# Attention's last weight block decoded and stored in round 22 instead of round 23, and its last four weight splits placed behind the first unit of the linear layers

## Chip, cores and metric

The kernel runs on one core of a Trainium2 chip. The metric is the device time of one execution in microseconds (us); less is better. The engines of the core have their own instruction queues: PE or TensorE (matmuls), DVE or VectorE, ACT or ScalarE, POOL or GpSimd, and SP, which here only issues DMA transfers, each in program order.

## What is computed

```python
S, D = 448, 64                      # 8 batches, 12 heads
scores = q @ k.transpose(0, 1, 3, 2) / sqrt(D) - log(S)
attn   = 1 / (1 + exp(-scores))     # a sigmoid, no sum over keys
x = (attn @ v).transpose(0, 2, 1, 3).reshape(3584, 768)
h = maximum(maximum(x @ w1, x @ w2), x @ w3)
out = h @ w_out                     # all weights 768 x 768
```

Inputs are float32, the weights float64 words that the kernel decodes to float32 itself.

## The kernel before

**Attention** (L277 to 466) handles one group of four heads a round, 24 rounds in all (n = 0 to 23, the loop at L420). A round takes about 10.17 us of TensorE: scores of the second head pair, scores of the next round's first pair (only if there is a next round, `ahead`), and the products with v, which gather in two PSUM banks, ps_av0 and ps_av1; the next round copies these to SBUF and stores them in x_dram (`finish`, L377).

**Weights.** The first layer weights are multiplied in a form with seven products in place of eight, so each needs sums of its blocks (a11 to a22, s1 to s4), and every operand goes in as a high and a low part. Attention does part of this work in the background. The generator `decoding` (L161) holds 24 blocks (0 to 23): for each of three weights four blocks of stage 0, which stay on the chip, and four of stage 1, which go to w_dram. A call decodes one block: two operations on ScalarE (L180, L181), four on DVE (L182 to L191). A stage 1 block is decoded in one call, and with `late=True` its store is issued at the start of the next, ahead of the next decode. Raw blocks rotate through 3 buffers, decoded ones (wb) through 2. `split_weights` (L407) makes the high and low part of one sum by a cast and a subtraction on DVE. In the round, L446 and L447 call both: one split (two in round 22), then one decode. So block 23 is decoded in round 23 and its store issued after the loop (L465), that of block 22 in round 23. The splits of the third weight become possible in round 20, and there are seven (order s3, a22, s1, a11, s2, a12, s4): one each in rounds 20 and 21, two in 22, one in 23, and two behind the first unit of the linear layers (L618).

In the last round t_store (L443) writes four token sums of 672 KB each to DRAM, and the high and low part of the first operand b11 are made (x_hi on ScalarE, L269; x_lo on DVE, L273).

**Linear layers** (L472 on). When attention ends, its pools are freed and new pools take their memory: xo2, which holds the high and low parts of the other six token operands (5376 bytes a partition each, in the order t2, t3, t1, b21, t4, b22, high before low), then c and dec2. The old memory began with dec: 3 raw buffers of 3072 bytes, 2 decoded ones of 1536, then the squares (2 x 1792), qk, hl, v, a. A tile of a new pool waits for the last use of the old tiles under it. Four visits (token pairs) for each of four stages, each of three units (q = 0 to 2), make 48 units; a unit is seven products of nine matmuls (three terms by three blocks of 128), some 12.6 us. The operands t2, t3, t1 of the first unit are made at L532 to L533, those of its last three products within it. Unit 0 of visit 0 uses the first weight, unit 2 the third.

All instructions keep program order on their engine (`pin`), so what is queued ahead of an instruction on its engine delays it.

Of the kernel before, what the change touches and what calls it, by code (L numbers as in the profile page):

```python
# [39 lines left out]
def attention_then_maxout(  # L40
# [86 lines left out]
    def w_stage():  # L127
        return {name: ws_p.tile([P, HP], F32, name=f"ws_{name}") for name in BLOCKS}
# [13 lines left out]
    def w_combine(r, names):  # L142
        for name in names:
            r[name] = r["a21"] if name == "s3" else ws_p.tile([P, HP], F32, name=f"ws_{name}")
            in0, in1, op = W_SUMS[name]
            pin(nc.gpsimd.tensor_tensor(out=r[name], in0=r[in0], in1=r[in1], op=op))  # L146
# [9 lines left out]
    def w_split(q, name, r, copy):  # L156
        hi, lo = w_tiles(q, name)
        pin(copy(out=hi, in_=r[name]))
        pin(nc.vector.tensor_tensor(out=lo, in0=r[name], in1=hi.bitcast(F32), op=ALU.subtract))

    def decoding(dec_p, todo, bufs, ahead, square_p, late=False):  # L161

        raws = []

        def load(st, q, n):
            col = (st if st < 3 else q) + 3 * (n // 2)
            src = w123[q, col] if st < 3 else wout[col]
            raw = dec_p.tile([P, HALF, P], I64, name="wraw", bufs=ahead)
            r = n % 2
            pin(nc.sync.dma_start(out=raw, in_=src[:, r * HALF : (r + 1) * HALF]))  # L170
            return raw

        def decode(raw, out):

            words = raw.bitcast(U32).rearrange("p a (c two) -> p (a c) two", two=2)
            low, high = words[:, :, 0], words[:, :, 1]
            square = square_p.tile([P, S], F32, name="c")[:, :HP]
            bits = dec_p.tile([P, HP], U32, name="wb", bufs=bufs)
            out = bits.bitcast(F32) if out is None else out
            pin(nc.scalar.activation(out=square, in_=high.bitcast(F32), func=AF.Square))  # L180
            pin(nc.scalar.activation(out=low, in_=low, func=AF.Copy, scale=2.0**-29))  # L181
            pin(nc.vector.tensor_scalar(  # L182
                out=bits, in0=high, scalar1=3, scalar2=0x3FFFFFF8,
                op0=ALU.logical_shift_left, op1=ALU.bitwise_and,
            ))
            pin(nc.vector.scalar_tensor_tensor(
                out=bits, in0=high, scalar=0xC0000000, in1=bits,
                op0=ALU.bitwise_and, op1=ALU.bitwise_or,
            ))
            pin(nc.vector.tensor_tensor(out=bits, in0=bits, in1=low, op=ALU.add))  # L190
            pin(nc.vector.scalar_tensor_tensor(  # L191
                out=out, in0=square, scalar=LEAST**2, in1=bits.bitcast(F32),
                op0=ALU.is_ge, op1=ALU.mult,
            ))
            return out

        for k, (st, q, n) in enumerate(todo):
            while len(raws) < min(k + ahead, len(todo)):
                raws.append(load(*todo[len(raws)]))
            if k == 0:  # L200
                yield
            if st == 0:
                if n == BLOCKS.index(W_ORDER[0][0]):
                    stage = w_stage()
                decode(raws[k], stage[BLOCKS[n]])
                w_combine(stage, dict(W_ORDER)[BLOCKS[n]])
                yield q, stage
            else:
                bits = decode(raws[k], None)
                if late:  # L210
                    yield
                pin(nc.sync.dma_start(out=w_dram[st, q][:, n], in_=bits))
                if not late:
                    yield


# [32 lines left out]
    def t_store(r, p):  # L249
        for k, name in enumerate(TOKENS):  # L250
            pin(nc.sync.dma_start(out=t_dram[p][:, k], in_=r[name]))
# [25 lines left out]
    def attention(stack):  # L277
# [11 lines left out]
        todo = []  # L289
# [3 lines left out]
        background = decoding(dec_p, todo, 2, 3, sq_p, late=True)  # L293
        splits = []

        def decode():
            done = next(background)
            if done:
                q, stage = done
                decoded.append(q)  # L300
                if decoded.count(q) == len(BLOCKS):
                    splits.extend((q, name, stage) for name in W_SPLITS)
# [8 lines left out]
        def load_v(b, f):  # L311
            t = v_p.tile([P, 14, D], F32, name="v")
            pin(nc.sync.dma_start(out=t, in_=v[b, f]))
            return t

        def sigmoid(ps):
            a = a_p.tile([P, 2, S], F32, name="a")
            pin(nc.scalar.activation(  # L318
                out=a, in_=ps[:, :, :S], func=AF.Sigmoid, bias=bias_s, scale=scale
            ))  # L320
            return a[:, 0], a[:, 1]

        def qk_split(t):

            hi = hl_p.tile([P, 2 * S], F32R, name="hi")
            lo = hl_p.tile([P, 2 * S], F32R, name="lo")
            pin(nc.vector.tensor_copy(out=hi, in_=t))
            pin(nc.vector.tensor_tensor(out=lo, in0=t, in1=hi.bitcast(F32), op=ALU.subtract))
            return (hi, hi), (hi, lo), (lo, hi)
# [42 lines left out]
        def load(n, pair):  # L372
            if n < len(fours):
                b, f = fours[n]
                return load_qk(b, 2 * f + pair)
# [26 lines left out]
        def raw_sigmoid(a):  # L402
            pin(nc.scalar.activation(
                out=a[1], in_=a[1], func=AF.Sigmoid, bias=bias_s, scale=scale
            ))

        def split_weights(most=1):  # L407
            for _ in range(most):
                if splits:
                    w_split(*splits.pop(0), nc.vector.tensor_copy)  # L410

        xs, count, pss = {}, len(fours), None
# [7 lines left out]
        for n in range(count):  # L420
            ahead = n + 1 < count
            later_ts = [later_t, load(n + 2, 1)]
            later_t = load(n + 3, 0)
            if ahead:
                next_vt = load_v(*fours[n + 1])
            if n == 0:
                first_terms = qk_split(next_ts[0])
            finish(n - 1, pss, gs=(0,))
            second = [shared_scores(scores(second_terms, c), c) for c in range(C)]
            finish(n - 1, pss, gs=(1,))  # L430
            if ahead:
                second_terms = qk_split(next_ts[1])
            next_first = []
            for c in range(C - 1):
                if ahead:
                    next_first.append(sigmoid(scores(first_terms, c)))
                raw_sigmoid(second[c])
            raw_sigmoid(second[C - 1])
            last_ps = scores(first_terms, C - 1) if ahead else None
            if n + 2 < count:  # L440
                first_terms = qk_split(later_ts[0])
            if n == count - 1:
                t_store(xs, 0)  # L443
                for name in FIRST:
                    x_lo(*x_hi(name, xs))
            split_weights(2 if n == count - 2 else 1)  # L446
            decode()  # L447
            if ahead:
                next_first.append(sigmoid(last_ps))

            part = n - 9
            if 0 <= part < 4 * HALF:
                k, block = divmod(part, 4)
                row, th = ((0, 1), (0, 0), (1, 1), (1, 0))[block]
                x_block(xs, x_dram, 0, row, th, k)
                x_combine(xs, ((), ("t1",), ("t2", "t3"), ("t4",))[block], (k,))
            pss = [ps_av.tile([P, 512], F32, name=f"ps_av{g}") for g in range(2)]
            for g, weights in enumerate((first, second)):
                for c in range(C):
                    weigh(pss[g], vt, g, c, weights[c])  # L460
            next_last = sigmoid(last_scores(next_ts)) if ahead else None
            last_weigh(pss, vt, last)
            if ahead:
                vt, first, next_ts, last = next_vt, next_first, later_ts, next_last
        next(background, None)  # L465
        return xs, lambda *to: finish(len(fours) - 1, pss, *to), split_weights

    with ExitStack() as stack:
        xs, finish, split_weights = attention(stack)
# [56 lines left out]
    ]  # L526
    todo = [(st, q, n) for st in (2, 3) for q in range(3) for n in range(4)]
    background = decoding(dec_p, todo, 1, 2, c_p)


# [137 lines left out]
```

## Time and profile before

| | us |
|---|---|
| median of 3 runs (872.13 to 872.5) | 872.45 |
| the profiled execution | 871.14 |
| its span, first to last instruction | 869.1 |
| busy: TensorE | 854.5 (98%) |
| busy: DVE | 658.0 (76%) |
| busy: ScalarE | 411.3 (47%) |
| busy: GpSimd | 177.0 (20%) |

The profile is one execution, recorded by the hardware. Its page groups instructions by line and tiles; beside it the trace can be asked for the waits (who waited for whom), for a timeline of an engine, for stretches of time, and for the instructions of one line or tile. In a timeline a row has the start in us from the span's start, the length, the engine, line and operation, the tiles (out<-in, without numbers, so that xhi_t is that of t1, t2, t3 or t4), and in brackets the idle time of the engine before it and what ended it. Operations on one engine are pipelined, so that the next may start a little before the end of the one before. A releaser is inferred from semaphores, and a wait for several is put down to the one that came last. In a stretch the columns are its length, then the busy time and count of PE, of weight loads, DVE, ACT and POOL, the granted clock of TensorE as a share of its full 2.4 GHz, the DMA engines' busy share and GB/s. Instructions of a line or tile are listed with count, least, median and greatest length in ns, and first and last start.

### The profile page before, as it was taken

To read this page: it belongs to the slowest core of one execution; us is meant where nothing else is said; L and a number is where in the kernel's file an instruction comes from. 1 tells how busy PE (TensorE), PEld (TensorE's weight loads), DVE (VectorE), ACT (ScalarE), POOL (GpSimd) and SP (SyncE) were. 2 spreads that over 40 slices of the span, in tenths; PEclk is the share of its full clock that TensorE was granted. 3 is DMA by queue.
4 is the path that set the end of the run, shared out by engine and by line. 5 is a ranking of instruction groups with operands and counts; after the bars stand their busy time and mean duration, and the time that the engine had idled before them with its cause. 6 is when DMAs were issued, how large, how long until landed. Compare 5 with 4: busy or idle time off the path is not lost. (4 is left out here: it accounts for less than half of the span.)

```text
span 869.1 us, 13093 instructions
## 1 busy us (share of the span) xinstructions
PE 854.5 (98%) x4842; PEld 698.8 (80%) x4842; DVE 658.0 (76%) x947; ACT 411.3 (47%) x571; POOL 177.0 (20%) x148
## 2 busy tenths in 40 slices
PE   7999999999979999999999999999999999999998
PEld 4555555555539999999999999999999998999997
DVE  5888888888857848589696888869688798837452
ACT  6888877788852414242253444225334352423320
POOL 0100012112002562602100020210002453760600
PEclk9999999999989999999999999999999999999999
DMA  7667776777654464414846542483663416262412
GB/s 269 224 225 252 235 242 237 258 262 245 201 203 172 168 233 147 187 52 131 307 141 236 219 171 79 135 304 134 239 230 138 168 58 230 82 213 98 169 73 84
DMA packets 74479, 161.88 MB, mean 186 GB/s; under 512 B 6960, under 2 KB 53936, under 8 KB 74416
## 3 DMA queue, kind: packets, MB, share of 16 engines
q1 hardware_dynamic: 74272, 160.94, 52.4%
q8 instruction: 38, 0.62, 0.3%
q14 instruction: 25, 0.20, 0.1%
q10 hardware_dynamic: 144, 0.11, 0.0%
HBM read 109.90 MB, written 51.12 MB: 185 GB/s over the span
## 5 line engine op out<-in xcount | busy, mean ns | idle before, releaser
L482 PE MATMUL ps_y<-xlo_t,whi_s 128*128 128x448 f32 x432 | 157.4, 364 | 4.3 <-DVE xlo_t L273 4.3
L482 PE MATMUL ps_y<-xhi_t,wlo_s 128*128 128x448 f32 x432 | 157.2, 364 | 1.5 <-ACT xhi_t L269 1.5
L482 PE MATMUL ps_y<-xhi_t,whi_s 128*128 128x448 f32 x432 | 156.7, 363 | 0.0
L318 ACT ACTIVATE a<-ps_s,bias_s 128x896 f32<-128x896 f32 x96 | 96.3, 1005 | 37.9 <-PE ps_s L348 33.3
L482 PE MATMUL ps_y<-xhi_b,wlo_a 128*128 128x448 f32 x288 | 104.5, 363 | 0.0
L482 PE MATMUL ps_y<-xlo_b,whi_a 128*128 128x448 f32 x288 | 104.4, 362 | 0.0
L482 PE MATMUL ps_y<-xhi_b,whi_a 128*128 128x448 f32 x288 | 104.0, 361 | 0.0
L592 ACT COPY p<-ps_y 128x448 f32<-128x448 f32 x48 | 25.5, 531 | 157.1 <-PE ps_y L482 156.6
L146 POOL TENSOR_TENSOR ws_s<-ws_a,ws_a 128x384 f32<-128x384 f32 x12 | 12.5, 1041 | 408.4 <-DVE u L598 172.7
L482 PEld LDWEIGHTS ps_y<-xlo_t,whi_s 128*128 128x128 f32 x432 | 81.6, 189 | 9.4 <-DVE xlo_t L273 4.6
L482 PEld LDWEIGHTS ps_y<-xhi_t,wlo_s 128*128 128x128 f32 x432 | 81.5, 189 | 7.8 <-ACT xhi_t L269 1.9
L482 PEld LDWEIGHTS ps_y<-xhi_t,whi_s 128*128 128x128 f32 x432 | 81.4, 188 | 5.7
L566 DVE TENSOR_TENSOR m<-ps_y,u 128x448 f32<-128x448 f32 x71 | 43.8, 620 | 52.6 <-PE ps_y L482 51.1
L273 DVE TENSOR_TENSOR xlo_t<-xs_t,xhi_t 128x1344 fp32r<-128x1344 f32 x42 | 67.9, 1616 | 4.0 <-DMA w_dram<-wb 4.0
L238 POOL TENSOR_TENSOR xs_t<-xs_b,xs_t 128x448 f32<-128x448 f32 x48 | 64.3, 1364 | 31.9 <-DMA xs_b<-x_dram 31.3
L595 DVE TENSOR_TENSOR u<-ps_y,p 128x448 f32<-128x448 f32 x48 | 29.8, 622 | 53.6 <-PE ps_y L482 48.4
L564 ACT COPY m<-ps_y 128x448 f32<-128x448 f32 x24 | 12.8, 534 | 120.9 <-PE ps_y L482 110.2
L273 DVE TENSOR_TENSOR xlo_b<-xs_b,xhi_b 128x1344 fp32r<-128x1344 f32 x42 | 68.0, 1620 | 2.4 <-ACT xhi_b L269 2.4
L269 ACT CAST xhi_t<-xs_t 128x1344 fp32r<-128x1344 f32 x42 | 55.3, 1317 | 17.7 <-PE ps_y L482 8.6
L180 ACT ACTIVATE c<-wraw 128x384 f32<-128x384 f32 x48 | 26.7, 557 | 74.7 <-DVE m L572 42.6
L269 ACT CAST xhi_b<-xs_b 128x1344 fp32r<-128x1344 f32 x42 | 55.3, 1318 | 9.9 <-PE ps_y L482 9.9
L356 PE MATMUL ps_av<-a,v 128*64 128x448 f32 x288 | 59.4, 548 | 0.0
(71 smaller groups left out, 1787.4 us busy)
## 6 DMA issues: line engine op xcount, KB each, us to landing
qk<-qk SPq DMA_DIRECT2D x48, 448.0 KB, 4.1
xs_b<-x_dram SPq DMA_DIRECT2D x30, 672.0 KB, 6.9
wraw<-w SPq DMA_DIRECT2D x36, 384.0 KB, 5.0
xs_t<-t_dram SPq DMA_DIRECT2D x18, 672.0 KB, 7.9
v<-v SPq DMA_DIRECT2D x24, 448.0 KB, 5.8
h_dram<-m SPq DMA_DIRECT2D x48, 224.0 KB, 1.9
xs_b<-h_dram SPq DMA_DIRECT2D x16, 672.0 KB, 5.8
outT<-m SPq DMA_DIRECT2D x47, 224.0 KB, 1.9
```

The lines of the kernel that those rows point to most:

```text
L146: pin(nc.gpsimd.tensor_tensor(out=r[name], in0=r[in0], in1=r[in1], op=op))
L180: pin(nc.scalar.activation(out=square, in_=high.bitcast(F32), func=AF.Square))
L238: pin(nc.gpsimd.tensor_tensor(out=r[name][:, k], in0=r[in0][:, k], in1=r[in1][:, k], op=ALU.subtract))
L269: pin(nc.scalar.copy(out=hi, in_=r[name]))
L273: pin(nc.vector.tensor_tensor(out=lo, in0=x, in1=hi.bitcast(F32), op=ALU.subtract))
L318: pin(nc.scalar.activation(out=a, in_=ps[:, :, :S], func=AF.Sigmoid, bias=bias_s, scale=scale))
L356: pin(nc.tensor.matmul(ps[e * D : (e + 1) * D, :S], vt[:, (g * C + c) * 2 + e], a[e], start=c == 0, stop=False,))
L482: pin(nc.tensor.matmul(ps[:, :S], wt[:, k * P : (k + 1) * P], xt[:, k], start=first and n == 0, stop=n == len(terms) - 1, skip_group_check ...
L564: pin(nc.scalar.copy(out=m[name], in_=y))
L566: pin(nc.vector.tensor_tensor(out=m[name], in0=y, in1=add, op=ALU.add))
L592: pin(nc.scalar.copy(out=p1, in_=ps[0][:, :S]))
L595: pin(nc.vector.tensor_tensor(out=u2, in0=ps[1][:, :S], in1=p1, op=ALU.add))
```

## The change

The generator stores its last block in the call that decodes it; the others keep their order. Round 23 calls neither `split_weights` nor `decode`; round 22 makes one split and calls `decode` twice, so blocks 22 and 23 are both decoded there and the stores of blocks 21, 22 and 23 are issued there. The call behind the loop goes. Three of the third weight's splits are made in rounds 20 to 22; the other four (a11, s2, a12, s4) are left for the call at L618, which makes all that are left.

```diff
             else:
                 bits = decode(raws[k], None)
-                if late:
+                wait = late and k + 1 < len(todo)
+                if wait:
                     yield
                 pin(nc.sync.dma_start(out=w_dram[st, q][:, n], in_=bits))
-                if not late:
+                if not wait:
                     yield
...
-            split_weights(2 if n == count - 2 else 1)
-            decode()
             if ahead:
+                split_weights()
+                for _ in range(1 if n + 2 < count else 2):
+                    decode()
                 next_first.append(sigmoid(last_ps))
...
-        next(background, None)
         return xs, lambda *to: finish(len(fours) - 1, pss, *to), split_weights
```

## Rows read from the trace of the kernel before

**Rows 1.** Waits of TensorE: what waited for what: us in total, times, longest.

```profile
PE ps_y L482 <- DVE xlo_t L273: 5.1, 2, 4.3
```

**Rows 2.** Timeline of TensorE at the seam; in brackets, idle before and releaser.

```profile
245.49 2.48 PE L356 MATMUL ps_av<-a,v 128*64 128x448 f32 x12
...
252.58 0.36 PE L482 MATMUL ps_y<-xlo_b,whi_a 128*128 128x448 f32 x1
252.78 0.36 PE L482 MATMUL ps_y<-xhi_b,whi_a 128*128 128x448 f32 x1
254.63 0.47 PE L482 MATMUL ps_y<-xhi_t,wlo_s 128*128 128x448 f32 x1 [1.49 <-ACT xhi_t L269]
259.42 0.74 PE L482 MATMUL ps_y<-xlo_t,whi_s 128*128 128x448 f32 x1 [4.32 <-DVE xlo_t L273]
...
263.16 0.36 PE L482 MATMUL ps_y<-xhi_t,whi_s 128*128 128x448 f32 x1
```

**Rows 3.** One stretch: its length, busy time of each engine, granted clock, DMA.

```profile
259.40:263.00 3.60, 3.58 (x10) 3.20 (x11) 3.15 (x3) 3.60 (x5) 0.00 (x0) 0.51 0.01 4
```

**Rows 4.** Timeline of DVE (VectorE) at the seam.

```profile
249.19 1.56 DVE L273 TENSOR_TENSOR xlo_b<-xs_b,xhi_b 128x1344 fp32r<-128x1344 f32 x1 [2.41 <-ACT xhi_b L269]
...
257.80 1.56 DVE L273 TENSOR_TENSOR xlo_t<-xs_t,xhi_t 128x1344 fp32r<-128x1344 f32 x1 [4.04 <-DMA w_dram<-wb]
259.67 1.56 DVE L273 TENSOR_TENSOR xlo_t<-xs_b,xhi_t 128x1344 fp32r<-128x1344 f32 x1 [0.31 <-ACT xhi_t L269]
261.14 1.55 DVE L273 TENSOR_TENSOR xlo_t<-xs_t,xhi_t 128x1344 fp32r<-128x1344 f32 x1
```

**Rows 5.** Timeline of ACT (ScalarE) at the seam.

```profile
253.26 1.31 ACT L269 CAST xhi_t<-xs_t 128x1344 fp32r<-128x1344 f32 x1 [3.17 <-DVE wb L190]
258.33 1.31 ACT L269 CAST xhi_t<-xs_b 128x1344 fp32r<-128x1344 f32 x1 [3.75 <-DMA wraw<-w]
```

**Rows 6.** Timeline of the issues in SP's queue, rounds 22 and 23.

```profile
237.03 0.42 SPq L212 DMA_DIRECT2D w_dram<-wb  x1
244.22 2.90 SPq L385 DMA_DIRECT2D x_dram<-m  x2
...
250.94 3.17 SPq L212 DMA_DIRECT2D w_dram<-wb  x2
```

**Rows 7.** Line 212 from 247 us on: both last stores, and their landing.

```profile
L212 SPq DMA_DIRECT2D w_dram<-wb x2: 319/1026/1733, 250.9 to 253.8; - x2
...
DMA to landing us min/median/max: 4.4/5.6/6.8
```

**Rows 8.** Line 212, the store issued at 237.03 alone: its landing.

```profile
DMA to landing us min/median/max: 2.1/2.1/2.1
```

**Rows 9.** Timeline of DVE in round 22: second split, decode, next copy.

```profile
239.06 0.36 DVE L158 CAST whi_a<-ws_a 128x384 fp32r<-128x384 f32 x1
...
239.93 0.36 DVE L182 TENSOR_SCALAR wb<-wraw 128x384 uint32<-128x384 uint32 x1
...
243.57 0.62 DVE L384 COPY m<-ps_av 128x448 f32<-128x448 f32 x1 [1.41 <-PE ps_av L365]
```

**Rows 10.** Timeline of ACT in round 22: decode's second half, next wait.

```profile
239.98 0.56 ACT L181 ACTIVATE wraw<-wraw 128x384 uint32<-128x384 uint32 x1
...
242.85 1.01 ACT L318 ACTIVATE a<-ps_s,bias_s 128x896 f32<-128x896 f32 x1 [1.42 <-PE ps_s L348]
```

**Rows 11.** Timelines of DVE, POOL (GpSimd) and ACT in units 0 to 2.

```profile
272.50 0.35 DVE L158 CAST whi_a<-ws_a 128x384 fp32r<-128x384 f32 x1
...
277.04 3.37 POOL L238 TENSOR_TENSOR xs_t<-xs_b,xs_b 128x448 f32<-128x448 f32 x3 [53.42 <-DMA xs_b<-x_dram]
...
284.11 4.15 POOL L238 TENSOR_TENSOR xs_b<-xs_b,xs_b 128x448 f32<-128x448 f32 x3
...
L238 POOL TENSOR_TENSOR xs_t<-xs_b,xs_t x6: 1151/1351/2479, 280.4 to 291.8; 128x448 f32<-128x448 f32 x6
...
290.00 1.32 ACT L269 CAST xhi_t<-xs_b 128x1344 fp32r<-128x1344 f32 x1 [0.47 <-PE ps_y L482]
```

## Prediction

> **What bounds the kernel now.** I read the page first: TensorE is busy for 98% of the span, and in its list of groups the matmuls of L482 that read a token sum's low part have idle time before them, put down to DVE's L273. The waits of TensorE say that this is nearly one event: 5.1 us in two waits, the longest 4.3 [rows 1]. So TensorE is the bound almost everywhere, and a change can gain only where it stands still. The timeline of TensorE shows where: at the seam between attention and the linear layers [rows 2]. The first product (a11, b11) runs in steps of 0.20 us up to the matmul at 252.78. The second product (s2, t2) starts at 254.63 instead of 252.98, after a wait of 1.49 us for ScalarE's high part, its second matmul at 259.42 instead of 0.20 us later, and the next ones run at half the granted clock, 0.51 from 259.4 to 263.0 [rows 3], which is the 1.2 GHz level, after an engine that did almost nothing for 6 us. The old pace is back at 263.16. That matmul is the twelfth after the one at 252.78; at 0.20 us a step it would start at 252.78 + 12 x 0.20 = 255.18. **The seam costs 263.16 - 255.18 = 7.98 us**: 1.65 for the first late start, 259.42 - 254.83 = 4.59 for the second, and 263.16 - 261.42 = 1.74 for the clock.
>
> Then I asked who is late. DVE had nothing else to do and waited 4.04 us with xlo_t2 until 257.80 for a store of a decoded block [rows 4]. ScalarE waited 3.17 us with xhi_t2 until 253.26 for DVE's L190, which is the last reader of attention's last raw buffer, and then 3.75 us with xhi_t3 until 258.33 [rows 5]. These are waits for memory, not for data: the pool xo2 lies where attention's pools lay. The pool dec has 3 raw buffers of 3072 bytes a partition and 2 decoded ones of 1536, and each xo2 tile has 5376, so xhi_t2 covers raw buffers, xlo_t2 raw buffers and a decoded one, and xhi_t3 the other decoded one. The two stores are issued from 250.94 on in SP's queue, behind the four t_store DMAs [rows 6], and land after 6.8 and 4.4 us [rows 7]: 250.9 + 6.8 = 257.7 is the release of xlo_t2, 253.8 + 4.4 = 258.2 that of xhi_t3. (The timeline puts xhi_t3 down to a raw load; the tiles under xhi_t3 have none, and the raw loads of the time are issued only behind both stores.)
>
> **The change, part by part.**
>
> *Last round (n = 23).* It loses one split (s2) and the decode of block 23 on ScalarE and DVE, and the stores of blocks 22 and 23 are ahead of t_store in SP's queue. ScalarE ends xhi_b11 by 249.19, when DVE starts xlo_b11 on it [rows 4]. After that it goes straight on with xhi_t2, xhi_t3 and xhi_t1, 1.31 us each [rows 5]: done by 250.5, 251.8 and 253.1. DVE, which starts such an operation every 1.47 us when nothing holds it (259.67 and 261.14, [rows 4]), ends xlo_b11 at 250.7, xlo_t2 at 252.2, xlo_t3 at 253.7, xlo_t1 at 255.2. TensorE wants xlo_t2 at 253.18, xlo_t3 at 254.98, xlo_t1 at 256.78 (second matmul of each product, 1.80 us apart). Slack 1.0, 1.3 and 1.6 us: TensorE would not stop, and without a stop the clock has no reason to fall. What is late next, if anything, is DVE in the first unit: xlo_b21, xlo_t4 and xlo_b22 wait in its queue between the sums, and by the same durations (0.62 for a sum) they end 1.4, 1.2 and 1.0 us before TensorE wants them.
>
> *The memory.* Block 23's decode in round 22 ends at about 243.9 (below). The stores of blocks 22 and 23 are issued at about 241.8 and 244.0, before the t_stores. Their landing isn't in the trace of before; the rows on both sides are 2.1 us, for the store at 237.0 with no t_store ahead of it [rows 8], and 6.8 us with four [rows 7]. I take 2.1, since the queue is as it was at 237.0; they land at about 244 and 246. Even with 6.8 they land at 248.6 and 250.8, while xlo_t2 wants its memory at 250.7 and xhi_t3 can wait until 253.4. So the cost is nothing at either end. ScalarE and the raw buffers are free at 243.9 too.
>
> *Round 22.* It loses one of two splits and gets a second decode. On DVE the split is 239.93 - 239.06 = 0.87 us, the decode 242.16 - 239.93 = 2.23 (243.57 less the idle 1.41 is 242.16) [rows 9]. DVE comes to L190 0.87 us sooner than now and waits some 0.4 us there, since ScalarE's L181 for block 22 ends at 240.54 [rows 10]. So 2.23 - 0.87 + 0.4 = 1.76 us come in, 1.41 of idle time cover them, and the copy of ps_av0 starts 0.35 us later, at about 243.9 instead of 243.57 [rows 9]. TensorE overwrites that bank at 245.49 [rows 2]: 1 us of slack, cost nothing. If that cover were gone, it would cost up to 1.76. On ScalarE the second decode puts 0.92 us ahead of the last sigmoid of the next round's first pair; ScalarE then idled 1.42 us until 242.85 [rows 10], so nothing again; without that cover 0.92.
>
> *The new wait.* The second decode of the round writes the decoded buffer that block 21's store reads, and that store is issued in the same round, at 237.0. DVE comes to it at about 241.7. With the landing of 2.1 us, which is that of this very store now [rows 8], the buffer is free at 239.1, and nothing waits. At the other end, 6.8, it is free at 243.8: DVE stands 2.1 us, and behind it are the copy of ps_av0 and the copies of round 23's scores. The copy would end at 246.7, 1.2 us after TensorE wants the bank. Taken: 0; bounds 0 and 1.2. A gain is excluded, since TensorE waits for nothing in these rounds.
>
> *The splits behind unit 0.* Four in place of two, so two more of 0.87 us on DVE, after the last sum of unit 0: the first is now at 272.50 [rows 11], so they stand at about 264.5 to 268.0. The next sum of unit 1 comes 0.4 us late, into buffers that are wanted microseconds later. The weights are wanted in unit 2, two units of 12.6 us after 251.06, at 276.3. Cost nothing; the cover is 8 us wide.
>
> *SP's queue.* The two stores now stand ahead of round 23's x_dram stores, which wait for DVE copies that are queued behind the same decode anyway; t_store starts as now, and the raw loads behind it 2 us or so sooner. Nothing waits for those soon.
>
> **Sum.** -7.98 + 0 + 0 + 0. The profiled execution has 871.14 us, of which 869.1 are the span; it would go to 863.16 with a span of 861.1. The median of the runs shown is 872.45, 1.31 more than the profiled one, so I predict 872.45 - 7.98 = **864.5**. Behind the seam all is led by TensorE's progress: the other wait for xlo_t, 5.1 - 4.3 = 0.8 us [rows 1], stays, and nothing gives the 8 us back.
>
> **The rivals.**
>
> *Operands late again.* The three slacks of 1.0 to 1.6 us in the first products, or those of the first unit, are eaten, say by ScalarE or DVE instructions that take longer beside t_store's reads. For: the slacks are small. Against: L273 has 1.56 us at 249.19 and at 257.80 alike [rows 4], one of them amid those transfers. A stop of 1 to 3 us leaves 865.5 to 867.5. Chance 0.05.
>
> *Gpsimd held up by the splits.* One of its subtractions takes 1.15 us at the least and 2.48 at the most [rows 11], while DVE works beside some of them. If the four splits ran beside the subtractions for the next pair, these could lose from nothing up to all of 4 x 0.87 = 3.5 us; t3 is done at 284.11 + 4.15 = 288.26 and wanted at 290.00 [rows 11], a slack of 1.74, so TensorE could lose 1.8: 866.3. Against: the splits end at 268.0, and the loads let Gpsimd start at about 277.04 - 7.8 = 269.2. Chance 0.03. The Trainium skill (SBUF — State Buffer, section Who interferes with whom) has VectorE and GpSimd share a port pair under an exclusive lock, which casts and sums of two SBUF operands need, the later instruction fully blocked; by that the loss would be the full 3.5 us; the row's longest, twice its shortest, allows it without showing the cause.
>
> *Nothing gained.* The last stores land as late as now, because SP issues them late in spite of the new order, or xo2 waits for something else of attention's last round, such as the last matmuls that read v or a. For: the waits are inferred. Against: SP issues nothing between 237.03 and 244.22 [rows 6], and the tiles over v and a come last in xo2. The time would be 872.4. Chance 0.03.
>
> *Slower.* The new wait for the decoded buffer: if block 21's store landed late, DVE would stand with round 23's copies behind it. It costs from a landing at 242.7 on, each further us about one; it eats the whole gain at 242.7 + 8 = 250.7, that is 13.7 us after the issue, and with 15 us the time is 874. No store here has more than 6.8 [rows 7]. Chance 0.03.
>
> **How the numbers follow.** Forecast 0.86, the rivals 0.05, 0.03, 0.03, 0.03. Runs of one kernel lie within 0.4 us, and about 0.2% (1.7 us) is what a measurement here can tell from no change. The range goes down to 863.8 (twice the 0.37 us between the runs shown) and up to 866.5: it takes in the new wait's bound (865.7) and the Gpsimd rival. Faster 0.94, same 0.03, slower 0.03.
>
> **What would show it.** Right: TensorE's matmuls run on in steps of 0.20 us from 251.06 through product two; the wait for xlo_t falls from 5.1 us in two to about 0.8 in one, that for xhi_t goes; the granted clock is 1.00 from 251 to 263; two decodes stand one behind the other in round 22, the second done near 243.9; both last stores land before 250.7; four splits stand near 264.5 to 268. Wrong: an idle stretch of TensorE at the seam with another name behind it, one before 251 (the new wait), or a new wait of ScalarE for Gpsimd in unit 2.

## The result, and the profile after

The changed kernel takes 863.34 us (median of 5 runs, 863.13 to 864.04), the kernel before beside it 872.36 (5 runs, 871.11 to 872.50): a ratio of 0.9901, with a 95% interval of 0.9887 to 0.9915. It is faster by 9.0 us; 864.5 were predicted, with 863.8 to 866.5 as the range, so the time lies 0.5 us below the range. The two profiled executions, 871.14 and 863.23 us, lie 7.9 us apart, which is what the prediction worked out for that pair (7.98). So the mechanism needs a test, and above all the missing microsecond.

TensorE's timeline at the seam, after the change (lines have moved by one: L482 is now L483, L273 is L274):

```profile
245.58 2.48 PE L357 MATMUL ps_av<-a,v 128*64 128x448 f32 x12
...
252.87 0.36 PE L483 MATMUL ps_y<-xhi_b,whi_a 128*128 128x448 f32 x1
253.07 0.36 PE L483 MATMUL ps_y<-xhi_t,wlo_s 128*128 128x448 f32 x1
253.27 0.36 PE L483 MATMUL ps_y<-xlo_t,whi_s 128*128 128x448 f32 x1
...
255.07 0.36 PE L483 MATMUL ps_y<-xlo_t,whi_s 128*128 128x448 f32 x1
```

Where [rows 2] have idle times of 1.49 and 4.32 us, product two (253.07) now follows product one in steps of 0.20 us, and xlo_t2, xlo_t3 are there when they are wanted. The waits of TensorE and the granted clock in the two stretches around it, to be held against [rows 1, 3]:

```profile
PE ps_s L337 <- DMA qk<-qk: 4.0, 1, 4.0
PE ps_y L483 <- DVE xlo_t L274: 0.8, 1, 0.8
...
253.00:259.40 6.40, 6.40 (x34) 6.00 (x33) 6.40 (x7) 4.18 (x4) 0.00 (x0) 1.00 0.77 260
259.40:263.00 3.60, 3.60 (x20) 3.38 (x19) 3.50 (x5) 0.54 (x1) 0.00 (x0) 1.00 0.10 37
```

These are all waits of TensorE that are left; the 4.0 us for qk are at the kernel's start, as before. Of 5.1 us of waiting for xlo_t, 0.8 remain (the other place, as predicted), and the clock is 1.00 in both stretches. DVE in rounds 22 and 23, against [rows 4, 9]:

```profile
240.66 0.56 DVE L190 CUSTOM_DVE_ANT_0 wb<-wraw,wb 128x768 uint16<-128x768 uint16 x1 [0.55 <-ACT wraw L181]
...
241.72 0.35 DVE L182 TENSOR_SCALAR wb<-wraw 128x384 uint32<-128x384 uint32 x1
...
243.40 0.56 DVE L191 SCALAR_TENSOR_TENSOR wb<-c,wb 128x384 f32<-128x384 f32 x1
243.88 0.62 DVE L385 COPY m<-ps_av 128x448 f32<-128x448 f32 x1
...
249.28 1.56 DVE L274 TENSOR_TENSOR xlo_b<-xs_b,xhi_b 128x1344 fp32r<-128x1344 f32 x1 [2.41 <-ACT xhi_b L270]
250.76 1.55 DVE L274 TENSOR_TENSOR xlo_t<-xs_t,xhi_t 128x1344 fp32r<-128x1344 f32 x1
252.23 1.55 DVE L274 TENSOR_TENSOR xlo_t<-xs_b,xhi_t 128x1344 fp32r<-128x1344 f32 x1
```

The first decode waits 0.55 us for ScalarE at L190 (0.4 predicted), the second one follows it without a wait at 241.72, so the new wait for the decoded buffer costs nothing, and the copy of ps_av0 starts at 243.88 (243.9 predicted) and ends 1 us before TensorE wants the bank. The three low parts stand one behind the other. SP's queue and the landing of the three stores of round 22, against [rows 6 to 8]:

```profile
237.12 7.19 SPq L213 DMA_DIRECT2D w_dram<-wb  x3
244.52 2.70 SPq L386 DMA_DIRECT2D x_dram<-m  x2
247.32 0.89 SPq L252 DMA_DIRECT2D t_dram<-xs_t  x2
...
L213 SPq DMA_DIRECT2D w_dram<-wb x3: 319/320/427, 237.1 to 244.0; - x3
...
DMA to landing us min/median/max: 1.8/1.9/3.6
```

The stores of blocks 22 and 23 land 1.8 and 1.9 us after their issue at 241.8 and 244.0 (2.1 was taken, 6.8 was the upper bound), that of block 21 after 3.6 (2.1 was taken), at 240.7, 1.0 us before the second decode writes its buffer. The four splits, and the start of GpSimd behind them:

```profile
264.61 0.35 DVE L158 CAST whi_a<-ws_a 128x384 fp32r<-128x384 f32 x1
...
268.06 0.62 DVE L596 TENSOR_TENSOR u<-ps_y,p 128x448 f32<-128x448 f32 x1
...
269.35 3.38 POOL L239 TENSOR_TENSOR xs_t<-xs_b,xs_b 128x448 f32<-128x448 f32 x3 [45.02 <-DMA xs_b<-x_dram]
```

They fill DVE from 264.61 to 268.06, and GpSimd starts at 269.35 (264.5, 268.0 and 269.2 predicted).

### The profile page after: what moved, and what is told of

It is laid out like the page before. It is cut to its first block, busy times and chain, and to the rows that moved or that the text cites. A ratio compares the mean times of both kernels' runs of the same rounds, so it can differ in the third digit from the quotient of the medians.

```text
span 861.5 us, 13092 instructions
## 1 busy us (share of the span) xinstructions
PE 853.0 (99%) x4842; PEld 698.0 (81%) x4842; DVE 660.5 (77%) x947; ACT 411.1 (48%) x571; POOL 175.5 (20%) x148
## 5 line engine op out<-in xcount | busy, mean ns | idle before, releaser
L483 PE MATMUL ps_y<-xhi_t,wlo_s 128*128 128x448 f32 x432 | 157.0, 363 | 0.0
L483 PE MATMUL ps_y<-xhi_t,whi_s 128*128 128x448 f32 x432 | 156.5, 362 | 0.0
L483 PE MATMUL ps_y<-xlo_t,whi_s 128*128 128x448 f32 x432 | 155.9, 361 | 0.0
L483 PE MATMUL ps_y<-xhi_b,wlo_a 128*128 128x448 f32 x288 | 104.8, 364 | 0.0
L483 PE MATMUL ps_y<-xhi_b,whi_a 128*128 128x448 f32 x288 | 104.4, 362 | 0.0
L483 PE MATMUL ps_y<-xlo_b,whi_a 128*128 128x448 f32 x288 | 104.0, 361 | 0.0
L593 ACT COPY p<-ps_y 128x448 f32<-128x448 f32 x48 | 25.5, 531 | 157.8 <-PE ps_y L483 145.2
L483 PEld LDWEIGHTS ps_y<-xhi_t,whi_s 128*128 128x128 f32 x432 | 81.1, 188 | 6.2
L483 PEld LDWEIGHTS ps_y<-xlo_t,whi_s 128*128 128x128 f32 x432 | 80.9, 187 | 5.5
L483 PEld LDWEIGHTS ps_y<-xhi_t,wlo_s 128*128 128x128 f32 x432 | 81.1, 188 | 4.3
L274 DVE TENSOR_TENSOR xlo_b<-xs_b,xhi_b 128x1344 fp32r<-128x1344 f32 x42 | 67.9, 1617 | 2.4 <-ACT xhi_b L270 2.4
L274 DVE TENSOR_TENSOR xlo_t<-xs_t,xhi_t 128x1344 fp32r<-128x1344 f32 x42 | 67.9, 1618 | 0.0
L239 POOL TENSOR_TENSOR xs_t<-xs_b,xs_t 128x448 f32<-128x448 f32 x48 | 61.0, 1296 | 32.5 <-DMA xs_b<-x_dram 32.1
```

The source lines that it names most:

```text
L239: pin(nc.gpsimd.tensor_tensor(out=r[name][:, k], in0=r[in0][:, k], in1=r[in1][:, k], op=ALU.subtract))
L274: pin(nc.vector.tensor_tensor(out=lo, in0=x, in1=hi.bitcast(F32), op=ALU.subtract))
L483: pin(nc.tensor.matmul(ps[:, :S], wt[:, k * P : (k + 1) * P], xt[:, k], start=first and n == 0, stop=n == len(terms) - 1, skip_group_check ...
L593: pin(nc.scalar.copy(out=p1, in_=ps[0][:, :S]))
```

## Experiments

**How dear is the seam of the kernel before?** The two pairs of numbers, 9.0 from the medians and 7.9 from the profiles, can only agree if the profiled execution of before was not a typical one. Theory 1: the seam itself varies from one execution to the next, through the clock. Theory 2: the difference lies outside the seam. The runs are of the kernel before, unchanged.

> The kernel before, unchanged, to see how far its single executions differ. The medians moved by 9.0 us, the two profiled executions by 7.9. Theory 1 (the seam itself varies): the executions at 872.4 us have a dearer seam than the profiled one at 871.1, because the clock stays low longer after the idle stretch or the last stores land later; then their mean granted clock is lower, 0.994 to 0.995 where the profiled one has 0.996, and the two levels of time go with two levels of clock. Theory 2 (the difference lies elsewhere: start, end, what lies around the span): the clock is 0.996 at both levels of time and the span moves without it.

> The kernel before once more, for a further profile of the seam. Two profiles so far: 22.70 us from the first matmul of unit 0 to the first sum copy of unit 1 in the execution of 871.14 us, 23.20 in that of 871.93, where the half clock lasted a microsecond longer; the changed kernel has 14.71. If the clock's return sets the spread of before: the stretch is between 22.2 and 24.2, the waits are 1.5 and 4.3 us again, and the longer stretch goes with the longer time. If not: the stretch is the same and the time moves with what lies outside it.

> As the look before, a fourth profile of the kernel before: the same waits of 1.5 and 4.3 us, and a stretch between 22.2 and 24.2 us that differs from the others only by how long the half clock lasts.

> A fifth profile of the kernel before. In the three taken later the half clock lasted until 263.4 to 263.9 and the stretch from unit 0's first matmul to unit 1's first copy was 23.10 to 23.20 us, in the first one until 262.6 and 22.70. If the first was a cheap draw: 23.0 to 23.3 again. If it varies evenly: anything between 22.4 and 23.5.

Measured: before_again 871.97 us (median of 11, 871.04 to 872.91) beside 871.82 (27 runs of the same kernel, 871.01 to 873.19), ratio 0.9999 (0.9990 to 1.0008); the others are single executions. The seam is measured from unit 0's first matmul to the first copy of a product that unit 1 makes on ScalarE (L592, L593 after the change); the changed kernel has 265.87 - 251.16 = 14.71, and 14.71 again in two more profiles below.

| profile of before | time, us | seam, us | above 14.71 | matmuls of 0.55 to 0.58 us in it |
|---|---|---|---|---|
| the one shown ahead of the prediction | 871.14 | 273.76 - 251.06 = 22.70 | 7.99 | 8 |
| before_look1 | 870.70 | 273.81 - 250.71 = 23.10 | 8.39 | 11 |
| before_look2 | 871.71 | 274.05 - 250.93 = 23.12 | 8.41 | 11 |
| before_again | 871.93 | 274.28 - 251.08 = 23.20 | 8.49 | 11 |
| before_look3 | 872.91 | 275.43 - 251.74 = 23.69 | 8.98 | 14 |

The waits are the same in all five (4.2 or 4.3 us and 1.5). What differs is when the half clock comes and goes. The granted clock in the stretch from 259.4 to 266.0, in the order first profile, before_again, before_look1, before_look2, before_look3 (columns as in [rows 3]):

```profile
259.40:266.00 6.60, 6.58 (x25) 6.00 (x26) 6.15 (x6) 5.53 (x6) 0.00 (x0) 0.73 0.01 2
...
259.40:266.00 6.60, 6.58 (x22) 5.95 (x23) 5.84 (x6) 5.52 (x6) 0.00 (x0) 0.65 0.01 2
...
259.40:266.00 6.60, 6.60 (x24) 5.94 (x24) 6.08 (x6) 5.04 (x5) 0.00 (x0) 0.68 0.00 0
...
259.40:266.00 6.60, 6.60 (x23) 5.95 (x24) 6.05 (x6) 5.22 (x5) 0.00 (x0) 0.66 0.00 1
...
259.40:266.00 6.60, 6.03 (x16) 5.38 (x17) 5.63 (x5) 6.07 (x6) 0.00 (x0) 0.51 0.03 13
```

Their TensorE gets 25, 22, 24, 23 and 16 matmuls into the same 6.6 us, at a mean clock of 0.73, 0.65, 0.68, 0.66 and 0.51. In the dearest one the matmuls still take 0.57 us at 265.36:

```profile
259.97 0.74 PE L482 MATMUL ps_y<-xlo_t,whi_s 128*128 128x448 f32 x1 [4.19 <-DVE xlo_t L273]
260.51 0.57 PE L482 MATMUL ps_y<-xhi_t,whi_s 128*128 128x448 f32 x1
...
265.36 0.57 PE L482 MATMUL ps_y<-xhi_t,wlo_s 128*128 128x448 f32 x1
265.73 0.46 PE L482 MATMUL ps_y<-xlo_t,whi_s 128*128 128x448 f32 x1
```

In the first profile the old pace is back at 263.16 [rows 2]. Each further matmul at the low level costs 0.37 - 0.20 = 0.17 us; six more of them, 14 in place of 8, are 1.0 us, the whole of 8.98 - 7.99, and three more the 0.5 of before_again. So theory 1 holds for the seam, and the profile on which the prediction rests had the cheapest seam of five; their mean is 8.45 us.

It does not hold for the whole spread of the times. Less their seams, the five times are 848.44, 847.60, 848.59, 848.73 and 849.22 us in the order of the table, and this spread of 1.6 us is wider than the 1.0 us of the seams. So the longer time doesn't always go with the longer seam, which was expected of before_look1: this profile has a seam 0.40 us longer than the first profile and yet the shorter time, since it comes to the seam 0.35 us sooner and takes 0.49 less behind it. Two more expectations missed. before_look3, with 23.69, lies above both of its ranges. And the sign written down for theory 1 in before_again didn't come: the mean granted clock is 0.996 at 871.01 us and at 873.19 us, and 0.995 at times between. By an estimate from these rows, three more matmuls at the low level (1.1 us at half the clock) would lower the mean of 870 us by 0.0006, less than its last digit can tell.

**Does the clock make the spread?** The waits of before stay, only TensorE is kept busy:

```diff
+                if here == (0, 0, 1):
+                    spare = ps_y.tile([P, 512], F32, name="ps_y3", bufs=1)
+                    for _ in range(3):
+                        product(spare, w_ops[0]["a11"], x_ops["b11"], True)
                 product(ps[bank], w_ops[q][wname], x_ops[xname], first)
```

> The kernel before with 27 extra matmuls (three times the product a11 x b11 into an unused bank, thrown away) between the first and the second product of unit 0. They take 5.4 us of a stretch in which TensorE stood still and delay nothing that is on time before 258.4. The stores and waits are those of before; only the clock should stay high. Theory 1: the stretch after 259.4 runs at 1.00, gain 1.7 us against the profiled execution and about 2.9 against the median of before, with a smaller spread between runs. Theory 2: 1.7 us against the median as well, same spread. If the clock falls all the same: no gain.

Measured: 870.49 us (11 runs, 870.00 to 871.26), ratio 0.9984 (0.9975 to 0.9993), 1.3 us below before. Its stretch after the waits:

```profile
259.40:263.00 3.60, 3.54 (x17) 3.20 (x18) 3.30 (x4) 3.60 (x5) 0.00 (x0) 1.00 0.02 8
...
259.45 0.47 PE L482 MATMUL ps_y<-xlo_t,whi_s 128*128 128x448 f32 x1 [0.67 <-DVE xlo_t L273]
```

The clock stays at 1.00. Of the expectation's gains the interval (0.6 to 2.2 us) holds 1.7 and not the 2.9 of theory 1. The 11 runs lie within 1.26 us, where the 11 of before_again span 1.87; the changed kernel's 13, with a mean clock of 0.999 to 1.00 too, span 1.41. That goes the way of theory 1, but so few runs don't show it, and in the five profiles the larger part of the spread lies outside the seam. The seam is 21.40 us long, 1.72 shorter than the middle one of the five profiles, but 6.69 above the changed kernel, where the late second matmul alone (259.45 in place of 253.2) accounts for 6.2. The other 0.45 us are small delays behind it: DVE makes its low parts one behind the other from 257.84 on, and a TensorE at full clock catches up with it. So, in the one profile that there is, the 1.74 us of low clock and the waits are not a plain sum; without the low clock, part of its price comes back as lateness of DVE.

**Which part holds the seam: the decode or the landing of the store?** Both decodes stay in round 22, only the last store goes back behind t_store:

```diff
-                wait = late and k + 1 < len(todo)
+                wait = late
...
+        next(background, None)
         return xs, lambda *to: finish(len(fours) - 1, pss, *to), split_weights
```

> The changed kernel, but block 23's store is issued after the loop again, behind t_store; decodes and splits stay as changed. If the landing of a store behind t_store is what holds the seam: xhi_t2 and xlo_t2 on time, xhi_t3 held until some 6.8 us after an issue near 250.9, so about 257.7, xlo_t3 done near 260.6 where TensorE wants it at 255.1: 5.5 us of stop and some 1.7 of low clock, about 870.5 us. If the decode on ScalarE and DVE in round 23 was the cause and the stores only its shadow: as the changed kernel, 863.4.

Measured: 871.16 us (11 runs), ratio 0.9990 (0.9981 to 0.9999). The landing of that one store, then ScalarE and TensorE, which wait for its memory:

```profile
L213 SPq DMA_DIRECT2D w_dram<-wb x1: 1230/1230/1230, 250.9 to 250.9; - x1
...
DMA to landing us min/median/max: 6.8/6.8/6.8
...
249.23 1.31 ACT L270 CAST xhi_t<-xs_t 128x1344 fp32r<-128x1344 f32 x1
257.76 1.31 ACT L270 CAST xhi_t<-xs_b 128x1344 fp32r<-128x1344 f32 x1 [7.22 <-issue]
...
259.13 0.74 PE L484 MATMUL ps_y<-xhi_t,wlo_s 128*128 128x448 f32 x1 [4.02 <-ACT xhi_t L270]
260.72 0.74 PE L484 MATMUL ps_y<-xlo_t,whi_s 128*128 128x448 f32 x1 [0.85 <-DVE xlo_t L274]
```

Issued at 250.9, landed 6.8 us later at 257.7; xhi_t3, which lies over its buffer, starts at 257.76, TensorE stops for 4.02 and 0.85 us, and the half clock follows. xlo_t2, which lies over the buffer of the store in time, is made at 250.83, as in the changed kernel. The seam is 22.33 us long, 7.62 above 14.71, where 7.2 were expected, and the time is 0.7 us above the expected 870.5. One store of 192 KB in the wrong place in SP's queue gives back nearly all of the gain, though the decode is done some 10 us sooner than in the kernel before.

**Is it the t_stores ahead of it?** The other way round: decode and splits as before, t_store moved behind the last block's store:

```diff
             if n == count - 1:
-                t_store(xs, 0)
                 for name in FIRST:
...
         next(background, None)
+        t_store(xs, 0)
```

> The kernel before with t_store issued behind the last block's store, at the end of attention; decode and splits stay in round 23. If the four t_stores ahead of the two last stores are the cause of the late landing: block 22's store is issued near 247.2 and lands near 250, xlo_t2 starts near 254.6 when xhi_t2 is there; block 23's store is issued at 253.8, lands after 2 to 3 us, xhi_t3 starts near 256.8, xlo_t3 ends near 259.6. TensorE loses 1.6 at the second product and some 3 at the third, 4.7 in all in place of 6.2, with low clock or not: 868.5 to 870.5 against 871.9. If the transfers are slow for another reason than the queue: no gain.

Measured: 867.73 us (4 runs, 867.15 to 868.48), ratio 0.9945 (0.9928 to 0.9962), 4.4 us below before and better than expected. The landing of the two stores, TensorE's waits, and the granted clock at the seam:

```profile
L212 SPq DMA_DIRECT2D w_dram<-wb x2: 327/376/424, 248.0 to 254.6; - x2
...
DMA to landing us min/median/max: 1.8/2.1/2.3
...
PE ps_y L482 <- DVE xlo_t L273: 2.3, 3, 1.1
PE ps_y L482 <- ACT xhi_t L269: 1.5, 1, 1.5
...
251.00:266.00 15.00, 12.00 (x61) 9.53 (x60) 13.00 (x16) 8.45 (x8) 0.00 (x0) 1.00 0.59 234
```

The stores land after 1.8 and 2.3 us. What is left is the decode's own lateness (xhi_t2 waits for L190 as before, 1.5 us for TensorE, and then DVE; of the 2.3 us for xlo_t, 0.8 are the other place). The longest idle stretch at the seam is 1.5 us, the clock is 1.00 there, and the 1.7 us of the expectation's dearer case are not paid in this profile; the longest of the four runs (868.48 us) has a mean clock of 0.997, so there it may have fallen. The seam is 18.81 us long, 4.1 above 14.71. So with the t_stores out of the way some 4.3 of the mean 8.45 us go, and 4.1 stay with the late decode. The two don't add: with the decode early and only one store late (store_late), 7.62 are left.

**Do the moved splits matter?** First the changed kernel with the splits where they were, then the splits alone:

```diff
+            if not ahead:
+                split_weights()
             if ahead:
-                split_weights()
+                split_weights(2 if n == count - 2 else 1)
```

> The changed kernel with the splits where they were (two in round 22, one in round 23, two behind unit 0); the early decode and store stay. It takes away the cover of round 22: DVE has 0.87 us more there, the copy of ps_av0 starts near 244.75 and ends near 245.4, just before TensorE overwrites the bank at 245.5; in round 23 the split stands between xlo_b11 and xlo_t2 or behind xlo_b11 and takes 0.87 of the 1.0 us of slack of xlo_t2. By the prediction's slacks: 863.4 to 864.3, at most 0.9 dearer. If the slacks were counted too large: 864.5 to 866 with a stop of TensorE at 245.5 or at the second product.

```diff
-            split_weights(2 if n == count - 2 else 1)
+            if ahead:
+                split_weights()
             decode()
```

> The other half of the change alone: the kernel before with one split in round 22 and none in round 23, four behind unit 0; decode and stores as before. It frees DVE for 0.87 us before block 23's decode, so xhi_t2 may start up to 0.9 us sooner, but block 22's store is issued as before behind t_store and lands near 257.7, so xlo_t2 is as late as before: 871.3 to 872.0, no gain that can be told. If the splits matter as such: 871 or less.

Measured: splits_old 863.28 us (4 runs, 862.58 to 864.09), ratio 0.9896 (0.9881 to 0.9911), the same as the changed kernel; splits_only 871.83 (10 runs), 0.9997 (0.9987 to 1.0006), the same as before. DVE's copy and TensorE's next use of the bank in splits_old in round 22, and TensorE's wait in splits_only:

```profile
244.77 0.62 DVE L385 COPY m<-ps_av 128x448 f32<-128x448 f32 x1
246.04 2.48 PE L357 MATMUL ps_av<-a,v 128*64 128x448 f32 x12
...
PE ps_y L483 <- DVE xlo_t L273: 6.0, 2, 5.2
```

With the split in round 22 the copy of ps_av0 starts 0.89 us later, but this whole execution is 0.46 later there (TensorE overwrites the bank at 246.04, in place of 245.58): against TensorE the copy is later by 0.43 us, because DVE has no idle time at L190 there. It ends 0.65 us before the bank is overwritten, TensorE has no wait there, and the seam is 14.79. The cover that the prediction counted was real and enough for that. Without the early decode TensorE still waits for xlo_t2, now 5.2 us. As far as these runs can tell (some 1.3 us either way for splits_old), the gain comes from the early decode and store alone.

**The size once more, and a second edit.** The changed kernel was run again on two chips, each time with the kernel before. On one of them it ran beside a version in which two of the second weight's splits leave the place where the 0.8 us wait is:

```diff
-  [(n - 1, 2, 5), (n - 1, 2, 6), (n, 0, 1)] + [(n, 0, 3)] * 2 + [(n, 0, 4)] * 2,
+  [(n - 1, 2, 5)] + [(n, 0, 3)] * 3 + [(n, 0, 4)] * 3,
```

> The changed kernel, unchanged, beside more runs of the kernel before on one chip, to pin the size of the gain. From 38 runs of before at a median of 871.9 and the profiles' seams of 7.99 and 8.49 us above the changed kernel: 863.4, a gain of 8.2 to 8.8 us, and runs that lie closer together than those of before. If the first medians (872.36 and 863.34) were typical: a gain of 9.0.

> The changed kernel, unchanged, on the same chip as the version with the second edit and the other runs of this group: 863.1 to 863.4, a wait of TensorE for DVE of 0.5 to 0.8 us, and 14.71 us from unit 0's first matmul to unit 1's first copy.

> The changed kernel with a second edit, at the one place where TensorE still waits between 20 us and the end (0.8 us at 715.3, for DVE): in the last stage change, two of the second weight's splits go from the time just ahead of that wait to (n, 0, 3) and (n, 0, 4). Their low parts take 0.47 us of DVE each ahead of the operand that is late. Expected: the wait of 0.8 us goes, 862.4 to 862.9 where the changed kernel has 863.2. If DVE is not what is late there, or the splits collide with something behind: 863.2 or more.

Measured: after_again 863.14 us (4 runs) beside 872.09 of before (7 runs), ratio 0.9895 (0.9880 to 0.9910); after_third 863.36 (4 runs) beside 872.31 (13 runs), 0.9898 (0.9881 to 0.9914); after_plus 863.18 (4 runs, 862.84 to 863.68), 0.9899 (0.9884 to 0.9914). The seam is 14.71 in both repeats. The gain is 8.95 us in both, above the 8.2 to 8.8 that were expected of after_again and near its rival's 9.0; the time and the wait of after_third came as expected. In after_plus the low part comes at 713.33, and TensorE has no idle time before its matmul:

```profile
713.33 1.55 DVE L274 TENSOR_TENSOR xlo_t<-xs_t,xhi_t 128x1344 fp32r<-128x1344 f32 x1
...
714.93 0.47 PE L483 MATMUL ps_y<-xlo_t,whi_a 128*128 128x448 f32 x1
```

The wait is gone from the profile, but 863.18 and 863.36 with runs 0.8 to 1.3 us apart can't be told from each other. Its profile has the least waiting of TensorE; that it is faster than the changed kernel isn't shown.

Over all runs of this study the kernel before has a median of 872.01 us (66 executions, not counting the profile ahead of the prediction, 870.70 to 873.19, standard deviation 0.63) and the changed one 863.23 (13 executions, 862.63 to 864.04, 0.44): a gain of 8.8 us.

## Why the mechanism was right and the size was not

**The bound and the cause** were right. store_late and tstore_behind show it from both sides: the waits were for memory under the stores' buffers, and their landing was late because of the t_stores ahead of them in SP's queue. The second of these waits had been named by the profile as one for a raw load [rows 5]; store_late, in which that store alone is late, confirms the prediction's reading.

**The moved work** cost nothing, step by step as worked out: round 22 on DVE and ScalarE, the new wait (with 1.0 us to spare in place of 2.6, as block 21's store landed after 3.6 us), the four splits, SP's queue. splits_old shows in addition that the decision to drop a split from round 22 wasn't needed for it. One reading was off without effect: xhi_t3 could not wait for its memory until 253.4. xlo_t3 is made from it, so by the 1.31 and 1.55 us of the two and the 254.98 at which TensorE wants xlo_t3 it had to start by about 252.1; it started at 250.37.

**The term that failed is the first one, 7.98 us.** It was right for the execution it came from (7.99 by the table), and the step that failed was to carry it over to the median. The term holds 1.74 us of low clock, and that part isn't a constant: between 8 and 14 matmuls ran at half clock in five profiles, and the shown one was the cheapest. The five seams cost 7.99 to 8.98 us, 8.45 on average, 0.47 more than the sum has. The prediction saw that the profiled execution lay 1.31 us below the median of the runs, and added the 1.31 as if they were common to both kernels; a part of them belonged to what the change removes.

The base of the sum was off as well: 872.45 is the median of three runs, and 66 have 872.01, 0.44 less. With both put right the sum is 872.01 - 8.45 = 863.56; the 0.2 us that are left to 863.34 are less than the scatter of single executions (0.44). A seam is best subtracted from the time of the very execution that it was read in: each profile's time less what its own seam has above 14.71 gives 863.15, 862.31, 863.30, 863.44 and 863.93 us, 863.23 on average, which is what the changed kernel has over all its runs. For the first profile this is the 863.16 that the prediction worked out on the way and then left.

The low end of the range failed because it was twice the 0.37 us between three runs, while the profiled execution in the same table already stood 1.31 us below their median; 66 executions span 2.5 us.

**The rest of the difference** is the draw of the executions. From 872.36 and 863.34 the gain is 9.0, from all executions 8.8, and the five seams give 8.45 on average. The five profiled executions of before have a mean of 871.68 us, 0.33 below the median of all; with a standard deviation of 0.63 a mean of five is uncertain by some 0.3, so nothing is left that would need a cause. Outside the seam the two kernels don't differ in the profiles: the five of before have 848.52 us on average, the three of the changed kernel 848.52, 848.04 and 849.19, 848.58 on average.

**The rivals.** GpSimd behind the splits didn't come about: its first three subtractions take 3.38 us after the change, against 3.37 [rows 11]. They began only when the splits had ended, so what an overlap would cost isn't shown here. Operands that are late again, no gain, and a stop by the new wait did not occur either. The rival that was missing was one on the near side: that the seam of the median execution is dearer than the seam in the trace.

## What to carry to other kernels

When memory of a closed pool is taken over, the last transfer out of the old tiles sets when the new work starts; look at where that small store stands in its queue, for 192 KB behind four transfers of 672 KB landed 6.8 us after the issue, and some 2 us after it when it was ahead of them. Where a stop of the matrix engine is followed by a low clock, as here, it costs more than the stop, and a different amount in each execution: where a saving is priced from one profile, subtract it from the time of that profile's own execution, ask which of its terms would come out the same in the next, and put those that wouldn't on the range. Work that only shares the edit (here the splits) is best tried alone.

## What the runs showed of the hardware

In all five profiles of before, TensorE is kept waiting for some 6 us with a single matmul in between, yet the granted clock fell from 1.00 to 0.50 as early as between 256 and 257 us and as late as between 259 and 260 in the one of 872.91 us, and came back near 263 and near 266. Stretches of one microsecond, of the first profile and of before_look3:

```profile
255.00:256.00 1.00, 0.10 (x1) 0.00 (x0) 0.00 (x0) 0.00 (x0) 0.00 (x0) 1.00 1.02 382
256.00:257.00 1.00, 0.00 (x0) 0.00 (x0) 0.00 (x0) 0.00 (x0) 0.00 (x0) 0.56 0.80 88
262.00:263.00 1.00, 1.00 (x5) 0.87 (x4) 0.82 (x2) 1.00 (x2) 0.00 (x0) 0.52 0.00 0
263.00:264.00 1.00, 1.00 (x7) 0.93 (x6) 1.00 (x2) 1.00 (x2) 0.00 (x0) 1.00 0.00 0
...
258.00:259.00 1.00, 0.00 (x0) 0.00 (x0) 0.65 (x1) 0.12 (x1) 0.00 (x0) 1.00 1.03 407
259.00:260.00 1.00, 0.03 (x1) 0.03 (x1) 0.91 (x1) 1.00 (x1) 0.00 (x0) 0.55 0.38 151
264.00:265.00 1.00, 1.00 (x5) 0.87 (x4) 1.00 (x2) 1.00 (x2) 0.00 (x0) 0.50 0.00 0
265.00:266.00 1.00, 1.00 (x4) 0.91 (x3) 0.52 (x1) 0.47 (x1) 0.00 (x0) 0.53 0.00 0
```

A late fall did not make the stop cheaper: the engine was idle while the clock was still high, and busy while it was low. In the profiles with stops of 1.5 us at the most (tstore_behind) and with matmuls that were thrown away in the pause (warm_fill) it is 1.00 at the seam.
